# Seven PSUM banks in one tile, waits per bank, and a newly searched order for attention mixed with a spectral filter

## The chip, the cores and the metric

The kernel runs on one core of a Trainium2 chip. Its time is the device time of one execution in microseconds. Times and traces are of the chip; the order in which instructions stand on an engine is read from the built programs, and no duration is taken from there.

## The reference

For one sequence x of 2048 tokens with 448 features, two branches are computed and mixed by a gate per token:

```python
g = sigmoid((x * gate_w).sum(-1, keepdims=True))
# branch A: attention with 16 heads of 28 features
q, k, v = split(x @ wqkv)
p = softmax(einsum("bhqd,bhkd->bhqk", q, k) * 28 ** -0.5)
a = merge_heads(einsum("bhqk,bhkd->bhqd", p, v)) @ wo
# branch B: a filter in the frequency domain
X = rfft2(x) * (w_r + 1j * w_i)
b = irfft2(X)
return g * a + (1 - g) * b
```

All inputs and the output are bf16; 16 x 2048 x 2048 exponentials are needed.

## The kernel before

**Attention.** The 16 heads form four quads g, and the 2048 queries four chunks c of 512: sixteen groups (g, c), taken one after the other. Within a group the 2048 keys are sixteen tiles kt of 128. A *unit* is one head of the quad with one key tile: a matmul of a 32-row tile of TensorE (32x512) that writes 128 keys x 512 queries of scores into one PSUM bank. The four heads of a quad sit on the four row tiles and may run side by side.

There are two ways from scores to weights. In the first (748 units), two units form a *step*: ScalarE (ACT) reads two neighbouring banks in one instruction of 1024 elements per partition and writes exponentials into a ring of 28 slots in SBUF (L1034). There are 374 of these. In the second (69 key tiles, with four units each), VectorE (DVE) adds a constant to the score and stores the sum as 16-bit integers, which are the bits of an approximate exponential (L993), and GpSimd (POOL) makes three copies with shifted bits (L1003); the four versions meet weighted copies of V. After either way, *quads* of four column-tiled matmuls (128x32 weights, 512 columns, pvb<-ring,vw or pvb<-pd,vd) add the product with V, and the row sums, into one bank of PSUM, pvb. At a group's end `normalise` copies pvb out, takes reciprocals, broadcasts them by a DMA through DRAM (rsc, Rb) or at the end by small matmuls, and scales.

**Everything else** runs on the same engines between: projections of q, k and V (xT, wpq, wpk), the transforms as matmuls with tables (CS, A, Bd), the multiplication with the filter (Wg, on DVE), the output projection and the gate (`background`, `out_tile`, `last_tile`).

**PSUM.** Of its eight banks, psA and psB have two each and take steps in turn: step i writes psA if i is even and psB otherwise, so its scores wait for exponential i-2. pvb has one. Three banks (bg) serve all other products by turns, the units for DVE among them; each of these is an `Item`, for which a table says which of the three it gets.

**The order.** The code makes an `Op` for each piece of work, and `run` emits them in the order of a stored table, which was searched beforehand; the engines take their instructions in that order, each engine in its own, and wait on semaphores. Due times and priorities in the code served the search only. Codes from 60000 on are *fillers*: four matmuls with a zero operand that add nothing to pvb. DMAs stand mostly on the queue of SyncE (SP), also in the table's order. All matmuls are recorded with the line of their helper (L432, transposes L435), DMAs with L407.

Of the kernel before, what the change touches and what calls it, by code (L numbers as in the profile page):

```python
# [29 lines left out]
UNITS = 128.0  # L30
# [8 lines left out]
    "eNoN1mNjWEsUQNHxnMG5SW2ltm3bNtPUtm3btm3bto3UdvveX9hf1jakJbHEkXCCJDqJQWKSWCQ2iUPikngkPiEkAUlIEpHEJAkJI0lJMpKc"  # L39
    "UJKCZCApSU6SiniSmuQijHQlQAKiCScZSRoiSXaSlkQlitQk6Ugmkp7UILVINZKNZCG5SVUSheQhWUkOUodkJiVJKRKNlCa1SV5SloSQUFKO"  # L40
    "1Cf5SH5SgBQiBUkxUp6UIRVJYVKEFCXFySZSgWwmlUgJ0oq0JVvIVrKStCPbyHayiqwmVcgOsoZMJGtJZTKJTCZTyFSyjqwnG0g3YpVXG8l0"
    "MoPMJLOIU7PJHDKX7CTziCDzySy/gCwkcWk8Gp8uIovJDL+ELCUJaEK6jKDaRRLRnqQxWU5WkECFqMQ0Ck1Co9JoNDqNQcNoTBqLxqZx6G6y"
    "h+wl+0ioak6iqqfkGXlOXpCXJILcIQ3IfhJJ7pID5B55RV6TKOo+eUMekI7kIXlEHpNo6iCJrqaRGKouOUSS0mQ0pupEYqnkNAU9TJ6Qt2SD"
    "j63ekfckjvpA4qp4qhc5Qo6SlDS+akGOkan0I/lEptHPpAlJoBKq6fQLSaS+Qip6nCRWJ0hqmkR9gxk0TH0lp8hpkoau8WnpGXKWJFX1SG9y"
    "jpwnF8hMepEkU61JOnqJXCZXyFVyjSRX18kNcpOkULfIbZKeplRlaAaakZ4kmWhinoSnUj+hLE2t0qhYvByNzcvTXxCNz/XpVFpVgX6H6Dy9"
    "oqYiHUQyqIzqG0nGm5HvJAaPyX+Qn6Qp+UUyqT+QWf2DSjSLyqo6k+okDk/OK9OGpArtSDvRuDwhX+ezqc60C82uEvD1PhEP439IUp5D/SX/"
    "CKGUMrrac9qV5lSCSqqoprkU0Kw0G81Oc9DcKif9TXLR3NRQS/PQPCovzUdTcEfzKk/z05keaUDj83wqhBagmWlBWogWpkVofpWFhtJ4vCgt"
    "RtuTNqQ47U4LqIw8E+9BS9Ke1PJCyhhtHC+oCqv0vIjiJgMvTaUppoqqtLy4siYlr0p70RKqGi2pqtNSKh0vrVJzYXrTUlSZYaSMKkHT8Bq0"
    "Jk3FmSmrsvFyipi/UF5l5dn5SFpB5eGjaEU1mlZSeXkOPobWopVVB/IbqqiqKhcfS535AdVUTg6mNq2ucvMaqh7tQurTBjQfr0NrKm9qqc+u"
    "MC/DG9J4Bk1dWlsV4XVUDNOI1FUFeEJTkNdTCUwjmpnXV1l4WV6IJzHFeQlegefnFXkDFcs0VDFNXFOTN1KNVWNandfg8U0TVZQnMk1VMhOY"  # L50
    "YryZim1K8lo8jglXIaa5qsRb08o8mklpWqgIVY6X5m1oW9qOtlItVXnenjbjrVUqE86/uaimB2mjEpsmtK1KbkJNO1WVN6XNeQQPM9X4F9de"
    "NeFNeQeV0Xx3P9xP98t1VN1oJ1WX1+MZTDjtoprT7qSz+u0iaBTzx1XhLWhX1ZK2591UJlOKd1cduPQ9lPLpTHrTU/VSrWhtXoeDN9763iqN"
    "6aNa8+imr3I+tRlMve+n0po2vL8aQtE34o35ABX4gSqFSWoym0FqKB1GB6shqi3/6xrwf244JZ76+rwdH6oa8qKG+WGqI2/FC5jhqqDpxkeo"
    "fIb7Qkb4kWqU6sU78eKmO89jSpjRKovpzceoljyr6UvGqh68Jw/xXXkLXsaE+qG8GR2n8prxqjOP7xP4YTyhH8wnqES+iBnC4/i4PrGfqPrQ"
    "SWqyym860C58iipsipmpKokP81F9NN+HT1PZTHRf2cTw09UMNVP15aVNH5LT9KWzVAqf0s9Wa30qH9PH8rF9at+PpvFlzRy1kKb1i+hiOosu"
    "oXPVUprOD+fzVDkzgvfn5c18NYYvUHfoXXqPrqD36QO6ki5UI+gq+pA+oo/pE7qarqFP6SI1lq+l6+h6uoEO4BvpM7pYae/5JjqOL1HP6Qu6"
    "mb6kkXQ8f0WXqtd0C91Kt9FBdDtdpsbT5WoCXaFWquV0IK9kNvoddBwdSEuZQTypX6WS+Yl0El2tZvI1ajKdzquZmmatGs1n8XVqvZrEa5iS"
    "pqLZoPrxyXwG36jm8lF8Np9CJ/A5fCTfpPrTWmYi36yqmwF0Hp/Ct6gKpoqparapZXyrmk13qCW8tgk3c+g0nstsV03MPLpTNTUr+HKewyzl"
    "u1Qzs1vN5xFmj1rE1/LspoVZyTfyxXw+3ac6mTw+r9+rxpCFPJ9fx/P7TfyAmkv3qwK+oG9r2pmD6pA6rPbwOqa1mcqbm728kD+idvBMfifP"
    "7LP4oyqr38wHkGPqFF1AT9Mz9Cw9R7P54+o8vUCz+xz+Ir1EL9MTajW/Qrfwq3QVv0av0xv0pKprbtJTah9fw7uaBby/6WNu0dv0jFrPT6vc"  # L60
    "Zj9vY97QKL6zOad20rNqF91N99DzagPfS/fR/fQAPUgP0QtqFz9Md/Mj9Cg9Ri+q43QZPUFP8kuqgzlJT/GO5hzfzi+ro/wYv6KuqlZmG+9h"
    "eprz/Dg/wa+pLia9v64y+BvqMK9nuptDPLk/wluam+qWus/7mduqgq/oe5mG5gG/o7byC/wir+Qr+7uqij/IQ3goz+jbmwO8kbmnBphu5r6q"
    "6h+om7yaf6j6mt7mPb3C39K7fKCpbx6pW/yxOs3P8idqmhllnqqrfDi5xO/xZ2qcGW/e0RfquXrCL/OyfqIp55/ya3y0eakiVRPfwLxSTf0Y"
    "81rd5s38ZPNGhfs7/AV/q5r7l/ydivAzTDFf3JfwJX0p38K/V/PNB9WflPaRfJB5xT+qT2q2iefL+Bv8DL/OJ5np5rP6ogabIeQRf8af88J+"
    "gvmqvqnH/Av/yhubsaaIf8inmO/qh+JMsE/8p/qlPvOpRjLFNBtK3vJ3/D3/rf6omWaO+av+8n98sVloiP7AP/J/SorlZpYhYoihWgmm+5Hh"
    "huvXfK5ZYRaZN/w3L+qFpuIPlzqnz+V/8G+8oVda6wXmO8/th5lGfpmJKn5y0L+40UvMPPM/SMLqbn6p8drpaMIK1N39SpOE9fA9fS8PLLro"
    "7QO9yYSxpGyECdGhOoZIxvr47aaxj6qFiKKTMycOmW2Gieg6mtYiVHgRQ4OIIraY3SamiCVi6h1mp6nuY+lAxNYJxFGTUMTRIWK/SSJQ1PBx"
    "dZjYZ/aYeDq+TqDjiaEmvqjla/s6vq6v51eZ1SaRSCzq+7giqWjgy/uEerOZ7deYRHqUH+3H+LE+sR7nx/sJfq+ZQE6aOT6JDtNpxFbT0ifV"
    "yXRynVa08W19O9/exxEXTAff0Y80KXRKvc7U9J38QdPKf6Cp9Ef6iaYTqXUanVwcM+nFZ5pWp9OpRGyRXp8xJ8xh84WmFhl0Rl1I7DKFRV/f"
    "z6cQ030ykUmfNwdMZp1FZ9U5RUqRS3T2XXwGsdYcN9l0PnHKZNcD/EA/yGcU+cVgP8Tn0Dl1EXHEFBWnTSaRS2cVQ/1Zk1vHYHl0NnHOxGTD"  # L70
    "fD6dV180XX1mEYtlEbFZft3f3zIFdEEdh2UXf+h685fmEHlEIb3BFNYlxT9aStwx5UURTVgFQVleUVQ/N7lFaXHJFNNTfHE91d8zZcRDU0KX"
    "1DXEffPAlNI1RWldQBQU70w8VkaXFa19OXHbxGfFxHBfVidgI3xCVk1UFIlYdVFOV9Dl9RNTQnyjE/1I/9J8pxV1FVFJ/6A/aRU9yVfWTQVj"
    "03xV8Ys+Mq9NNV1c1Bdf6TNTVTcQv+ld89hU1zV0LVFbTPZPTU0dwmrpSiLSGNZMWPbFvDDzfG093y/wdfRCX1fU0+lZBpaRZWJ1tWOhLAqL"
    "yj6YuOyjWeQvm/o6GsvMGosGuol4axrphnoEaShasEainqgsWrJWrDVrwxKztqwda8+ysSO+sc7OOrAlfqPJwXKyXOyKaaKb6twsD8vLOrJO"
# [1396 lines left out]
```

## Time and profile before

| | |
|---|---|
| median of 3 runs | 380.9 us (380.81 to 381.44) |
| span of the profiled execution | 379.2 us (its time with what lies around the span is not given) |
| granted TensorE clock | 1.000 |
| PE busy | 371.3 us (98%) |
| ACT busy | 351.1 us (93%); the recorded lengths of the 374 exponentials, which overlap, add up to 403.4 us |
| DVE busy | 339.1 us (89%) |
| POOL busy | 234.4 us (62%) |
| first exponential, start of the last | 12.74 us, 364.96 us |

A busy PE includes matmuls whose ends are modelled, so its 98% does not say that it could take nothing more. The length of an exponential in the trace (1.02 us and more) is longer than the distance to the next one, since consecutive ones overlap; its pace is read from starts. A row of the timeline gives start, duration, engine, line, operation, output, inputs and count, and in brackets the idle time before it and what ended that.

### The profile page before, as it was taken

Reading aid. Unit: us, or ns where it says so; the run is one execution under the profiler, and the core shown is the slowest. Engines: PE = TensorE matmul, PEld = TensorE weight load, DVE = VectorE, ACT = ScalarE, POOL = GpSimd, SP = SyncE. Lnnn points to the kernel's source line nnn. Section 1 sums busy time; section 2 is a strip of 40 time slices with the busy share of each in tenths; the row PEclk is TensorE's granted clock in tenths of the full one; section 3 lists DMA queues with packets and bytes.
Section 4 is the critical chain, followed back from the end, with each engine's and each line's share of the span. In section 5 each row is a group of like instructions: output and inputs, shape, how many; then the busy total and the mean of one; then the engine's idle time right before and its main releaser. Section 6 shows DMA issues by size and latency. Waiting matters only on the chain.

```text
span 379.2 us, 12643 instructions
## 1 busy us (share of the span) xinstructions
PE 371.3 (98%) x5117; PEld 142.4 (38%) x5117; DVE 339.1 (89%) x665; ACT 351.1 (93%) x389; POOL 234.4 (62%) x264
## 2 busy tenths in 40 slices
PE   8999999999999999999999999999999999999996
PEld 6634223342433333234333434233333323433564
DVE  1768899999999999999999999999999999988744
ACT  2799999999999999999999999999999999999841
POOL 4446465866778866565553565778597778483510
PEclk9999999999999999999999999999999999999999
DMA  6511101010210112211322212223222122222132
GB/s 145 157 34 44 29 18 36 4 36 2 41 52 22 44 41 54 55 38 30 68 60 93 69 40 49 57 61 70 45 64 74 30 69 72 86 64 72 35 103 75
DMA packets 31158, 21.23 MB, mean 56 GB/s; under 512 B 16260, under 2 KB 29052, under 8 KB 31100
## 3 DMA queue, kind: packets, MB, share of 16 engines
q1 hardware_dynamic: 29708, 19.96, 20.7%
q8 instruction: 40, 0.66, 0.7%
q10 hardware_dynamic: 1392, 0.46, 0.5%
q14 instruction: 18, 0.15, 0.1%
HBM read 14.51 MB, written 1.96 MB: 43 GB/s over the span
## 4 chain that ended last, share of the span: by engine, by line
PE 55%; ACT 31%; issue 6%; DVE 4%; DMA 2%; POOL 1%; SPq 0%; DVEq 0%; ACTq 0%; POOLq 0%
ACT ring L1034 31%; PE bg L432 24%; PE pvb L432 17%; PE psA L432 7%; PE psB L432 6%; DVE pd L993 2%; PE bg L435 1%; DMA CS<-cCS 1%; DVE X L1419 1%; POOL pd L1003 1%; DMA Wg<-in_B_w_i_dram 0%; DVE X L1298 0%; DVE q L1178 0%; DVE t L1362 0%; DVE wpq L1224 0%
## 5 line engine op out<-in xcount | busy, mean ns | idle before, releaser
L1003 POOL INT64_ADD pd<-pd x207 | 211.9, 1038 | 96.7 <-DVE pd L993 27.4
L1034 ACT ACTIVATE ring<-psA 128x1024 bf16<-128x1024 f32 x187 | 201.7, 1078 | 4.7 <-PE psA L432 3.2
L1034 ACT ACTIVATE ring<-psB 128x1024 bf16<-128x1024 f32 x187 | 201.7, 1079 | 2.6 <-PE psA L432 1.4
L993 DVE TENSOR_SCALAR pd<-bg 128x512 uint16<-128x512 f32 x276 | 180.9, 681 | 8.5 <-PE bg L432 3.5
L432 PE MATMUL pvb<-pd,vd 128*32 128x512 bf16 x1104 | 96.9, 384 | 0.1
L432 PE MATMUL bg<-q,k 32*128 32x512 bf16 x276 | 96.3, 383 | 0.2
L432 PEld LDWEIGHTS <-k 32*128 32x128 bf16 x1024 | 40.1, 91 | 122.4 <-issue 117.7
L432 PE MATMUL psB<-q,k 32*128 32x512 bf16 x374 | 73.2, 383 | 1.3 <-ACT ring L1034 0.7
L432 PE MATMUL psA<-q,k 32*128 32x512 bf16 x374 | 72.8, 383 | 0.5 <-ACT ring L1034 0.2
L432 PE MATMUL pvb<-ring,vw 128*32 128x512 bf16 x748 | 67.9, 384 | 0.0
L432 PEld LDWEIGHTS <-vd 128*32 128x32 bf16 x1104 | 25.3, 94 | 35.5 <-issue 31.1
L432 PEld LDWEIGHTS <-vw 128*32 128x32 bf16 x748 | 17.5, 94 | 22.7 <-issue 20.5
L432 PEld LDWEIGHTS <-xT 128*128 128x128 bf16 (+5 forms) x512 | 20.3, 97 | 10.7 <-issue 9.7
L432 PE MATMUL bg<-xT,wpq 128*32 128x512 bf16 (+3 forms) x244 | 21.2, 383 | 0.1
L1362 DVE TENSOR_TENSOR t<-bg,Wg 128x450 bf16<-128x450 f32 x32 | 18.8, 614 | 0.6 <-DMA Wg<-in_B_w_i_dram 0.4
L432 PE MATMUL bg<-xT,wpk 128*32 128x512 bf16 (+2 forms) x240 | 18.9, 383 | 0.0
L432 PE MATMUL bg<-wvr,xT 128*128 128x112 bf16 (+2 forms) x192 | 13.7, 213 | 0.0
L1178 DVE TENSOR_TENSOR q<-pvs,Rb 128x512 bf16<-128x512 f32 x15 | 10.9, 729 | 2.6 <-DMA Rb<-rsc 2.6
L1298 DVE TENSOR_TENSOR X<-bg,oc 128x226 bf16<-128x226 f32 (+1 forms) x32 | 12.3, 386 | 0.5
L432 PEld LDWEIGHTS <-CS 128*32 128x32 bf16 x384 | 9.0, 95 | 9.9 <-issue 5.6
L432 PE MATMUL bg<-xtok,CS 128*32 128x225 bf16 (+1 forms) x192 | 11.2, 294 | 0.7 <-DMA CS<-cCS 0.7
L742 DVE TENSOR_SCALAR k<-bg 128x512 bf16<-128x512 f32 x15 | 10.3, 685 | 1.3 <-PE bg L432 1.1
(117 smaller groups left out, 315.4 us busy)
## 6 DMA issues: line engine op xcount, KB each, us to landing
Rb<-rsc SPq DMA_DIRECT2D x60, 64.0 KB
CS<-cCS SPq DMA_DIRECT2D x16, 192.0 KB
V<-xtok SPq DMA_DIRECT2D x16, 113.0 KB
Wg<-in_B_w_i_dram SPq DMA_DIRECT2D x64, 28.1 KB
xtok<-Ab SPq DMA_DIRECT2D x16, 112.5 KB
xtok<-in_A_x_dram SPq DMA_DIRECT2D x3, 448.0 KB
Wg<-in_B_w_r_dram SPq DMA_DIRECT2D x32, 28.1 KB
out_dram<-wpq SPq DMA_DIRECT2D x6, 112.0 KB
```

The lines of the kernel that those rows point to most:

```text
L432: self.pin(self.nc.tensor.matmul(out, lhsT=lhsT, rhs=rhs, start=start, stop=stop, **kw))
L435: self.pin(self.nc.tensor.transpose(out=out, in_=in_, identity=self.c("ident")[0:n, 0:n]))
L742: self.pin(nc.vector.tensor_scalar(out=dst, in0=self.bgi(it), scalar1=SQ, scalar2=None, op0=ALU.mult))
L993: self.pin(nc.vector.tensor_scalar(out=ys[:, s, :].bitcast(U16), in0=self.bgi(it), scalar1=127 * UNITS, scalar2=0.0, op0=ALU.add, op1=ALU. ...
L1003: self.pin(nc.gpsimd.int64_add(out=fl(pds), in0=fl(ys), in1=PHASE[f] * 0x0001000100010001))
L1034: self.pin(nc.scalar.activation(out=self.ring[:, u0:u0 + len(st), :], in_=slot[:, 0:len(st), :], func=ACT.Exp, scale=LN2 / UNITS))
L1178: e = self.dve(dv(512), lambda: self.pin(nc.vector.tensor_tensor(out=dst, in0=pvs[:], in1=self.Rb[:], op=ALU.mult)), ds, kk, lk=True)
L1298: self.pin(nc.vector.tensor_tensor(out=free_dims(self.X1[:, t, :], [[F, 2], [-1 if dif else 1, n]], (F - 1) * dif), in0=free_dims(self.bgi ...
L1362: self.pin(nc.vector.tensor_tensor(out=out[:], in0=self.bgi(it)[:, 0:F2].rearrange("p (a f) -> p a f", a=2), in1=free_dims(Wg[:], [[F, 2], ...
L1419: self.pin(nc.vector.tensor_tensor(out=free_dims(self.zt[0:FN], [[128, 4], [1, 128]], 512 * t), in0=self.bgi(it)[0:FN, :].rearrange("p (a ...
```

## The change

psA, psB and the three bg banks become one tile, `ps`, of seven banks. Each score unit is now an `Op` with an `Item` of its own, and the table gives it any of the seven banks; the two units of a step must get two neighbouring banks, in either order, and if the second has the lower bank, their slots in the ring are swapped. Since all seven are now one tile, `pin` notes which banks an instruction uses and declares that it does not depend on instructions that use other banks only, unless its `Op` names them as producers. The table has three more parts: the width of each step (2 for all 374), and for each of DVE's key tiles how its four units are grouped: 53 tiles stay at four operations of 512, in 16 one pair of units in neighbouring banks is done by one operation of 1024. The order of all operations and the banks are new. There are no fillers left. The homes of the prologue's products are banks from the table too, and the output tiles 12 and 13 no longer wait by rule for the last exponentials.

The table (a line of each kernel stands for all):

```diff
 TABLE = (
-    "eNoN1mNjWEsUQNHxnMG5SW2ltm3bNtPUtm3btm3bto3UdvveX9hf1jakJbHEkXCCJDqJQWKSWCQ2iUPikngkPiEkAUlIEpHEJAkJI0lJMpKc"
...
+    "eNpjYhoF9AcAJW4C7Q==",
...
 def unpack(table):
     raw = [zlib.decompress(base64.b64decode(t)) for t in table]
-    return np.frombuffer(raw[0], np.uint16).tolist(), np.frombuffer(raw[1], np.uint8).tolist()
+    return [np.frombuffer(r, t).tolist() for r, t in zip(raw, (np.uint16, np.uint8, np.uint8, np.uint8))]
...
+    def need(self):
+        return [p for d in self.op_now.deps for p in d.made]
...
     def run(self, filler):
         items = [o.acq for o in self.ops if o.acq is not None]
-        codes, banks = unpack(TABLE)
-        for it, b in zip(items, banks):
+        assert len(items) == len(self.banks)
+        for it, b in zip(items, self.banks):
             it.bank = b
-        for c in codes:
+        for c in self.codes:
             if c < FILL0:
+                self.used, self.op_now = set(), self.ops[c]
                 self.ops[c].emit()
+                self.used = set()
...
     def pin(self, ins):
...
+        if self.sc.used:
+            used = frozenset(self.sc.used)
+            keep = [p for p, u in self.sc.need() if not used & u]
+            if ins.ins.engine in self.before:
+                keep.append(self.before[ins.ins.engine])
+            for other in self.bank_sets:
+                if not used & other:
+                    self.tc.declare_no_dep(ins.ins, group="bank" + repr(sorted(other)), reason="other banks",
+                                           keep=[k for k in keep if k.name in self.bank_sets[other]])
+            self.bank_sets.setdefault(used, set()).add(ins.ins.name)
+            self.tc.add_to_no_dep_group("bank" + repr(sorted(used)), ins.ins)
+            self.sc.op_now.made.append((ins.ins, used))
+        self.before[ins.ins.engine] = ins.ins
         return ins
...
-        self.psA = ps.tile([P, 2, 512], F32, name="psA")
-        self.psB = ps.tile([P, 2, 512], F32, name="psB")
+        self.ps = ps.tile([P, 7, 512], F32, name="ps")
         self.pv = ps.tile([P, 512], F32, name="pvb")
-        self.bgt = [ps.tile([P, 512], F32, name=f"bg{i}") for i in range(3)]
...
     def bgi(self, item, dt=F32):
-        t = self.bgt[item.bank][:]
+        t = self.ps[:, item.bank, :]
+        self.sc.used.add(item.bank)
         return t if dt == F32 else t.bitcast(dt)
...
+            for part in self.PARTS[sc.parts[di]]:
...
+                def f1(part=part, its=its, ys=ys, at=at):
+                    bs = sorted(it.bank for it in its)
+                    sc.used.update(bs)
+                    w, e = len(bs), part[-1] - part[0]
+                    assert w == 1 or bs[1] == bs[0] + 1
+                    if its[0].bank > its[-1].bank:
+                        at[part[0]], at[part[1]] = part[1], part[0]
+                    self.pin(nc.vector.tensor_scalar(
+                        out=free_dims(ys[:], [[512 * e, w], [1, 512]], 512 * part[0]).bitcast(U16),
+                        in0=self.ps[:, bs[0]:bs[0] + w, :],
+                        scalar1=127 * UNITS, scalar2=0.0, op0=ALU.add, op1=ALU.max))
...
         for i, st in enumerate(self.steps):
-            slot = self.psA if i % 2 == 0 else self.psB
-            deps = [exps[i - 2]] if i >= 2 else []
+            deps, ms = [], []
...
-            def fe(st=st, slot=slot, u0=u0):
-                self.pin(nc.scalar.activation(out=self.ring[:, u0:u0 + len(st), :], in_=slot[:, 0:len(st), :],
+            def fe(st=st, u0=u0):
+                us = sorted(st, key=lambda u: uit[u].bank)
+                bs = [uit[u].bank for u in us]
+                assert all(b == bs[0] + j for j, b in enumerate(bs))
+                self.sc.used.update(bs)
+                for u, slot in zip(us, sorted(self.unit_slot[u] for u in us)):
+                    self.unit_slot[u] = slot
+                self.pin(nc.scalar.activation(out=self.ring[:, u0:u0 + len(st), :],
+                                              in_=self.ps[:, bs[0]:bs[0] + len(st), :],
                                               func=ACT.Exp, scale=LN2 / UNITS))
```

In the changed kernel the helper's lines are L464 (matmul), L467 (transpose) and L439 (DMA), DVE's approximate exponential is L1025. Three places show how the order moved. The first is PE around the 162nd exponential, where projections, the transform and attention run together; q_85, k_89 and vw_91 before are q_81, k_85 and vw_87 now, and ps stands for any of the seven banks. Before:

```order
L432 LDWEIGHTS k_89
L432 MATMUL bg_65<-q_85,k_89 128x512
L432 LDWEIGHTS k_89
L432 MATMUL psB<-q_85,k_89 128x512
...
L432 MATMUL psA<-q_85,k_89 128x512
...
L432 LDWEIGHTS vw_91
L432 MATMUL pvb<-ring,vw_91 32x512
```

Now:

```order
L464 MATMUL pvb<-ring,vw_87 32x512
L464 LDWEIGHTS k_85
L464 MATMUL ps<-q_81,k_85 128x512
...
L464 LDWEIGHTS A
L464 MATMUL ps<-X_127,A 32x450
```

Both visits have five score units, four for ACT and one for DVE: before, DVE's comes first, then psB's two and psA's two; now the two of one step, DVE's unit, and the two of the next. What follows moved from a product with V to a piece of the transform.

The second is DVE in the stage where the filter is applied, with a merged operation; t and Z are the filter's products, pd the approximate exponentials. Before:

```order
L1369 TENSOR_TENSOR Z_149<-t_147 128x225
L1367 TENSOR_TENSOR Z_149<-t_145 128x225
L993 TENSOR_SCALAR pd_107<-bg_65 128x512
L1362 TENSOR_TENSOR t_144<-bg_64,Wg_142 128x450
L1362 TENSOR_TENSOR t_146<-bg_64,Wg_142 128x450
L993 TENSOR_SCALAR pd_111<-bg_66 128x512
```

Now:

```order
L1408 TENSOR_TENSOR Z_144<-t_142 128x225
L1406 TENSOR_TENSOR Z_144<-t_140 128x225
L1025 TENSOR_SCALAR pd_104<-ps 128x512
L1025 TENSOR_SCALAR pd_109<-ps 128x1024
L1025 TENSOR_SCALAR pd_109<-ps 128x512
```

Two of four units of the key tile that pd_109 holds are done in one operation, between units of another key tile.

The third is SP's queue at the last loads of the transform's table CS; Wg is the filter, rsc and Rb the reciprocals of a group. Before:

```order
L407 DMA Wg_142<-in_B_w_r_dram 64x1x225
L407 DMA Wg_143<-in_B_w_r_dram 64x1x225
L407 DMA CS_140<-cCS 128x768
L407 DMA Wg_142<-in_B_w_i_dram 64x1x225
L407 DMA CS_141<-cCS 128x768
L407 DMA Rb<-rsc_128 32x512 x2
```

Now:

```order
L439 DMA Wg_139<-in_B_w_r_dram 64x1x225
L439 DMA CS_136<-cCS 128x768
L439 DMA Wg_138<-in_B_w_i_dram 64x1x225
L439 DMA Wg_139<-in_B_w_i_dram 64x1x225
L439 DMA rsc_124<-rr_102 128x16
L439 DMA CS_137<-cCS 128x768
```

The loads of Wg still stand ahead of the first CS; between the two CS there are now another Wg load and the store of the reciprocals.

297 lines of the change are left out of this document (151 added, 146 removed).

## The prediction

> **What bounds the kernel now.** I read the span in seven stages first: for each stage its length, then the busy time of PE, PEld, DVE, ACT and POOL with instruction counts, the granted clock, the share of the DMA engines and GB/s.
>
> ```profile
> 12.70:28.50 15.80, 15.72 (x202) 7.17 (x204) 11.63 (x22) 14.92 (x19) 6.16 (x10) 1.00 0.21 49
> 28.50:50.70 22.20, 22.17 (x274) 7.30 (x266) 19.38 (x38) 22.20 (x27) 13.15 (x23) 1.00 0.12 31
> 50.70:153.80 103.10, 102.27 (x1421) 35.36 (x1417) 99.98 (x198) 103.06 (x114) 75.11 (x77) 1.00 0.13 33
> 153.80:201.40 47.60, 47.60 (x684) 17.46 (x677) 46.28 (x90) 44.95 (x50) 26.29 (x27) 1.00 0.21 51
> 201.40:341.90 140.50, 138.24 (x1801) 49.16 (x1802) 135.52 (x276) 140.19 (x154) 98.03 (x98) 1.00 0.25 63
> 341.90:366.00 24.10, 24.10 (x452) 11.16 (x448) 16.13 (x26) 20.94 (x23) 9.23 (x9) 1.00 0.24 69
> 366.00:379.20 13.20, 9.67 (x244) 7.02 (x236) 6.80 (x12) 1.55 (x2) 0.00 (x0) 0.99 0.22 72
> ```
>
> No engine bounds all of it. ACT, which computes the 374 exponentials, is idle for 0.00, 0.04 and 0.31 us in the second, third and fifth stage: 266 of the 379 us in which nothing on PE, DVE or POOL can shorten the run unless ACT itself has less to do. PE has no idle time in the fourth and sixth stage, and ACT has 2.65 and 3.16 us there (the length less its busy time). In the first ACT misses 0.88 us. The last 13.2 us have no exponential; there PE and what hangs on it count. The clock is full throughout, so it explains nothing.
>
> Next, what ends ACT's waits (line, what it waited for: us in all, times, longest), and the same for PE's score matmuls.
>
> ```profile
> ACT ring L1034 <- PE psA L432: 4.5, 8, 0.8
> ACT ring L1034 <- PE psB L432: 2.5, 6, 0.6
> ...
> PE psB L432 <- ACT ring L1034: 0.7, 2, 0.4
> ...
> PE psA L432 <- ACT ring L1034: 0.2, 1, 0.2
> ```
>
> So ACT waits 7.0 us for scores, but PE waits only 0.9 us for an exponential to give a score bank back. Scores are late because PE is at other work, not because a bank is missing. Two of ACT's waits, and the last ones, in its timeline (start, duration, and in brackets the idle time before it and what ended it):
>
> ```profile
> 161.44 1.08 ACT L1034 ACTIVATE ring<-psA 128x1024 bf16<-128x1024 f32 x1
> 162.85 1.02 ACT L1034 ACTIVATE ring<-psB 128x1024 bf16<-128x1024 f32 x1 [0.32 <-PE psB L432]
> 163.77 1.02 ACT L1034 ACTIVATE ring<-psA 128x1024 bf16<-128x1024 f32 x1
> ...
> 361.50 1.02 ACT L1034 ACTIVATE ring<-psA 128x1024 bf16<-128x1024 f32 x1 [0.69 <-PE psA L432]
> 362.42 1.02 ACT L1034 ACTIVATE ring<-psB 128x1024 bf16<-128x1024 f32 x1
> 364.04 1.02 ACT L1034 ACTIVATE ring<-psA 128x1024 bf16<-128x1024 f32 x1 [0.61 <-PE psA L432]
> 364.96 1.02 ACT L1034 ACTIVATE ring<-psB 128x1024 bf16<-128x1024 f32 x1
> ```
>
> An undisturbed exponential follows its predecessor after 0.92 us (362.42 less 361.50); the one at 162.85 came after 1.41. Last, the chain that ended last, whose shares confirm the picture: about half PE, a third ACT.
>
> ```profile
> PE 55%; ACT 31%; issue 6%; DVE 4%; DMA 2%; POOL 1%; SPq 0%; DVEq 0%; ACTq 0%; POOLq 0%
> ```
>
> **The base of the sum.** The page gives this execution's span, 379.2 us, and no time around it; the median of the three runs is 380.9. I change the span and add the 1.7 us between the two again.
>
> **Part 1, PE's work.** The exponentials are the same 374 of 1024 elements, POOL's copies the same 207, and the matmuls that compute are the same; PE loses only the 24 zero matmuls of six fillers. What the new order changes is how the row-tiled score units (32x512) alternate with the column-tiled rest. PE's timeline prices it:
>
> ```profile
> 160.24 0.40 PE L432 MATMUL pvb<-ring,vw 128*32 128x512 bf16 x4
> 160.47 0.39 PE L432 MATMUL bg<-xT,wpq 128*32 128x512 bf16 x4
> 160.79 0.39 PE L432 MATMUL psA<-q,k 32*128 32x512 bf16 x2
> 160.85 0.37 PE L432 MATMUL bg<-q,k 32*128 32x512 bf16 x1
> 161.15 0.40 PE L432 MATMUL pvb<-pd,vd 128*32 128x512 bf16 x4
> 161.38 0.39 PE L432 MATMUL bg<-xT,wpq 128*32 128x512 bf16 x4
> ```
>
> A column quad follows a column quad after 0.23 us (160.24 to 160.47, 161.15 to 161.38), a score round follows a quad after 0.32 (160.47 to 160.79), and a quad follows a score round after 0.30 to 0.36. A change of mode therefore costs 0.10 us. Counted from the two orders, changes of mode fall from 717 to 691 (26 x 0.10 = 2.6 us), rounds of score units from 387 to 379 (8 x 0.22 = 1.8 us), and the fillers take 0.6 to 1.6 us, bounded by half of a quad's 0.22 and by their recorded length:
>
> ```profile
> L432 PE MATMUL pvb<-zero x24: 219/259/283, 251.3 to 277.9; 128*32 128x256 bf16 x12, 128*32 128x192 bf16 x8, 128*32 128x128 bf16 x4
> ```
>
> (six quads by 0.10 or 0.26). PE gains 5.0 to 6.0 us; I take 5.4. What matters is where. I counted rounds and changes between the same exponentials in both orders and priced them as above: about 1.1 us go before 50 us, 0.3 comes in between 50 and 154, nothing changes between 154 and 201, 4.0 go between 201 and 342, and 0.7 go from the 351st exponential to the end. (These are sums of counts by the starts above, no runs.) The 4.0 lie in the stage where ACT has 0.31 us of idle time. They are worth at most that.
>
> **Part 2, the heavy stage (153.8 to 201.4).** PE is full and its work stays the same. The possible gain is all of ACT's idle time, 2.65 us, if PE could be ahead of ACT when the stage begins; the possible loss comes with part 4. What seven interchangeable banks give directly is that a score unit need not wait for the exponential before the last. That wait is 0.9 us in the whole trace. I take 0.4 of it as gained, half, since by the table of banks 580 of the 744 units still take over a bank that the exponential two before gave back, and only 27 one that an older exponential did.
>
> **Part 3, head, transfer wait and tail.** In the head one exponential is late by 0.8 us because a block of projections stands before its scores; the new order has such a block there too. I count 0, and keep 0.9 either way. At 305 us PE waits for a table of the transform (chain of waits, then ACT's timeline):
>
> ```profile
> 301.95 3.92 DMA CS<-cCS
> 305.91 0.69 PE bg L432 x5
> ...
> 305.34 1.12 ACT L1034 ACTIVATE ring<-psB 128x1024 bf16<-128x1024 f32 x1
> 306.74 1.02 ACT L1034 ACTIVATE ring<-psA 128x1024 bf16<-128x1024 f32 x1 [0.28 <-PE psA L432]
> ```
>
> The exponential came 1.40 after its predecessor instead of 0.92: 0.5 us. SP issues in order, and this transfer stands behind a run of filter loads. In the new order it is still behind seven or more of them, but from the release of its buffer to its use there are now 4 exponentials, not 3: about 3.7 us against a transfer of 3.9. So it may be just late still. I take 0.2 of the 0.5. The tail: the work left on PE after the last score falls from 10.7 to 9.8 us by the same count, and from the 351st exponential on from 34.3 to 33.6. PE bounds here and it ends the chain, so I take 0.7; the bounds are 0 (the gaps of the last 13.2 us, 3.5, grow by as much) and 1.6 (half of these gaps go too).
>
> **Part 4, the exponentials on DVE.** 16 of 69 key tiles have one pair of 512-wide operations merged into one of 1024. From DVE's timeline:
>
> ```profile
> 120.55 0.68 DVE L993 TENSOR_SCALAR pd<-bg 128x512 uint16<-128x512 f32 x1
> 121.15 0.38 DVE L1298 TENSOR_TENSOR X<-bg,oc 128x224 bf16<-128x224 f32 x1
> 121.45 0.24 DVE L1169 RECIPROCAL rr<-rs 128x16 f32<-128x16 f32 x1
> ```
>
> 512 elements hold DVE for 0.60 us (120.55 to 121.15), 224 for 0.30, so 288 more cost 0.30 and 512 more about 0.53: a merged one 1.13 instead of 1.20, 0.07 saved, or 1.1 us for all sixteen. The bounds are 0 and 0.60 each (9.6 us), the first since the pair can at worst cost twice one. The skill's "Perfetto Trace Analysis", Optimizing Scalar/DVE Operations, puts the fixed part of a DVE operation on PSUM at about 125 ns; by that sixteen merges save 2.0 us. Either is off the path wherever ACT bounds, and is cover lost where it matters: both units must be there before it starts, and the first bank comes free 0.53 us later. 131 of the 744 score units of the exponentials now take a bank that DVE read last; before it was 2. Where DVE is late, PE waits with everything behind it, since its instructions are in order: other scores, the products with V, and the transform. DVE is busy 46.28 of 47.60 us in the heavy stage, so it has no slack to speak of there. For the likeliest case I count 0: laid end to end with the durations above, DVE's results that come less than 0.2 us ahead of the PE instruction that needs them are 22 in the new order and 17 in the old, few among some hundreds. The loss is the second rival.
>
> **Sum.** 0.4 (banks) + 0.2 (transfer) + 0.7 (tail) + 0.1 (what ACT can still gain in its own stages, a third of 0.31) = 1.4 us. 379.2 - 1.4 + 1.7 = 379.5 us, with 378.0 to 380.1 as this case's own range.
>
> **Rivals.** (a) *No change.* The tail's 0.7 goes into its gaps and ACT's 7 us stay where PE is full. For it: no stage in which PE bounds has less of the work but the tail. Against: the tail's order is really shorter by 0.9 us at the end. It gives 380.7, and all from 380.1 to 381.7, 0.2% either side, which a measurement of this kernel can't tell from no change.
>
> (b) *Slower: scores wait for DVE.* The place is the two stages in which PE is full, 153.8 to 201.4 and 341.9 to 366.0; 71.7 of the 352 us in which exponentials run, so about 27 of the 131 units. A unit that comes while DVE is at the operation before its own waits between 0 and 0.60 us, 0.3 in the mean; PE passes it on one to one, as it has no idle time. A third of the 27 being late costs 2.7, all of them 8.1. From five late units on (5 x 0.3 = 1.5) the gain is gone. With 13 late: 379.5 + 3.9 = 383.4; with a third, 382.2. For it: DVE's 97% in that stage, and the merges, which hold a bank longer. Also the work of PE between two scores is less even in the new order in the heavy stage and the tail, which makes ACT wait where there was no wait. Against: the order places a unit on a DVE bank mostly where DVE read long before. I take 382.3 for this case.
>
> (c) *The whole of ACT's waits.* If the scores came early enough everywhere, ACT's 0.88, 2.65, 0.31 and 3.16 us would go, 7.0, and the tail's 0.7: 373.2; with half of the waits, 376.7. For it: any of seven banks can take a score while both earlier exponentials run. Against: PE is busy 47.60 of 47.60 there, and no bank gives it time. "Perfetto Trace Analysis" of the Trainium skill, Optimizing Tensor Performance, wants independent matmul groups rotated through different PSUM banks, so that evacuation overlaps the next group, and under Matmul Optimizations all 8 banks used; by it (c) is the case, while the row of PE's waits (0.9 us) says the overlap is there already.
>
> (d) *The waits aren't per bank.* If each instruction waited for the last one on the whole tile, an exponential could not run beside the next scores, and its 0.92 would grow by a score's 0.39: 374 x 0.39 = 146 us, 527 in all. The wait lists of the changed order name single earlier instructions, so 0.01.
>
> **Chances.** Forecast 0.36, (a) 0.28, (b) 0.25, (c) 0.10, (d) 0.01. Faster by over 0.2% (below 380.1) is forecast and (c), 0.46; within it 0.28; slower (over 381.7) 0.26. The range: down to 376.2, which leaves the better half of (c) out, and up to 383.2, beyond a late third of the units and near 13 late ones.
>
> **What would show it.** Right: ACT's waits for scores still 5 to 7 us and in the same two stages; PE with more idle time between 201 and 342 us and that stage as long as before; the last exponential within a microsecond of 366.0 and the end 12.5 us after; DVE's operation of 1024 taking 1.1 to 1.2 us. Wrong: waits of PE for DVE on score units beyond 1 us in all, or the stage 153.8 to 201.4 longer (b); that stage at 46 us or less, and the last exponentials without gaps (c). The forecast fails most easily if the small gaps of the heavy stage, which depend on the neighbours of each score and not on sums, close or open throughout.

## The result and the profile after

The changed kernel takes 393.9 us (393.52 to 394.31), the kernel before beside it 380.86: a ratio of 1.0343 (95% interval 1.0328 to 1.0357), 13.0 us slower. 379.5 had been forecast, and the range ended at 383.2. The profiled execution's span is 392.1 us instead of 379.2. Two of e6's four runs below, 408.3 and 408.8 us, lie over 1.5% above its fastest and are left out of its time and ratio.

The page of the changed kernel, first two parts:

```profile
PE 372.6 (95%) x5093; PEld 142.9 (36%) x5093; DVE 347.5 (89%) x649; ACT 353.3 (90%) x389; POOL 235.1 (60%) x264
...
PEclk9999899999999999999799999999999999999998
```

No engine has more work to speak of but DVE, with 8.4 us more in fewer instructions (649 for 665). And the granted clock, full throughout before, now falls in two places, besides the very end. What ACT and PE waited for (line, what for: us, times, longest):

```profile
ACT ring L1075 <- PE ps L464: 17.4, 24, 3.3
...
PE ps L464 <- DVE pd L1025: 2.8, 9, 0.7
PE pvb L464 <- DVE vd L914: 2.2, 1, 2.2
PE ps L464 <- DVE vt L905: 1.8, 1, 1.8
PE ps L464 <- ACT ring L1075: 1.7, 5, 0.5
```

ACT waits 17.4 us for scores, 7.0 before. PE, which waited 0.2 us for DVE before, now waits 6.8 in the three groups shown, and two single waits make 4.0 of that.

The starts of the exponentials, read from ACT's timeline of both kernels and numbered from 0, say where the time went:

| from number to number | before, us | after, us | difference |
|---|---|---|---|
| 5 to 29 | 22.48 | 22.82 | +0.34 |
| 29 to 34 | 4.51 | 9.45 | **+4.94** |
| 34 to 60 | 23.78 | 23.80 | 0.0 |
| 60 to 152 | 84.84 | 86.76 | +1.92 |
| 152 to 175 | 22.63 | 22.59 | 0.0 |
| 175 to 180 | 4.56 | 9.01 | **+4.45** |
| 180 to 204 | 24.27 | 24.42 | +0.15 |
| 204 to 310 | 97.25 | 98.46 | +1.21 |
| 310 to 340 | 28.29 | 27.50 | -0.79 |
| 340 to 373 | 34.12 | 34.61 | +0.49 |
| 373 to the end | 14.23 | 14.16 | -0.07 |

(Number 5 starts at 18.23 us before and at 18.48 now.) Two stretches of five exponentials hold 9.4 of the 13 us. In stages (length, busy time of PE, PEld, DVE, ACT, POOL, clock, DMA share, GB/s) they are the second and the fourth row:

```profile
11.70:41.00 29.30, 26.57 (x339) 12.04 (x335) 22.45 (x40) 26.79 (x32) 13.56 (x25) 1.00 0.23 59
41.00:50.30 9.30, 6.48 (x66) 1.92 (x64) 6.93 (x10) 4.78 (x6) 3.32 (x8) 0.82 0.01 3
50.30:178.00 127.70, 125.77 (x1725) 42.05 (x1722) 122.75 (x233) 126.12 (x139) 83.39 (x86) 1.00 0.13 34
178.00:194.00 16.00, 14.24 (x164) 5.76 (x156) 14.25 (x23) 11.66 (x14) 8.79 (x9) 0.79 0.14 37
...
212.00:352.00 140.00, 135.56 (x1758) 48.88 (x1747) 136.41 (x265) 139.13 (x153) 97.96 (x100) 1.00 0.23 64
```

At the first place, PE's timeline of the changed kernel (start, duration, what; idle time before it in brackets):

```profile
40.76 0.39 PE L464 MATMUL ps<-q,k 32*128 32x512 bf16 x2
43.36 0.40 PE L464 MATMUL pvb<-pd,vd 128*32 128x512 bf16 x4 [2.21 <-DVE vd L914]
...
46.45 1.93 PE L464 MATMUL ps<-xT,wpq 128*32 128x512 bf16 x16
...
49.22 1.04 PE L464 MATMUL ps<-xT,wpq 128*32 128x512 bf16 x16
```

DVE's timeline of the same time:

```profile
38.35 0.61 DVE L905 TENSOR_TENSOR vt<-ps,w 128x448 f32<-128x448 f32 x1
39.07 4.24 DVE L914 TENSOR_SCALAR vd<-vt 128x580 bf16<-128x580 f32 x1
43.23 1.27 DVE L1025 TENSOR_SCALAR pd<-ps 128x512 uint16<-128x512 f32 x2
```

And POOL's:

```profile
38.96 0.37 POOL L557 COPY wpq<-X 96x224 bf16<-96x224 bf16 x1
39.30 2.05 POOL L1039 INT64_ADD pd<-pd  x2
41.30 0.37 POOL L557 COPY wpk<-X 96x224 bf16<-96x224 bf16 x1
41.65 1.03 POOL L1039 INT64_ADD pd<-pd  x1
42.62 0.37 POOL L554 COPY wpk<-X 128x224 bf16<-128x224 bf16 x1
42.94 0.60 POOL L554 COPY wpq<-X 128x224 bf16<-128x224 bf16 x1
43.49 0.24 POOL L843 CAST vw<-w 128x16 bf16<-128x16 f32 x1
```

One DVE operation, a scaling of V from SBUF to SBUF (vd<-vt), takes 4.24 us; of the other fifteen of the same shape twelve take 0.44 to 0.47, and three 0.66 to 1.30. It ends at 43.31 us, in the last 0.4 us of a row of POOL's operations that has had no gap since 35.64. PE waits 2.2 us for it. Sixteen matmuls that take 1.04 us at 49.22 took 1.93 at 46.45: between them the clock was half. At 184 us it is the same with other operations: products of the transform (Z) take 1.1 us each instead of 0.27, and the queries' scaling takes 1.5 instead of 0.7, all during a row of POOL's copies; PE waits 1.8 us, and from 185.2 to 192.0 its clock is half.

Before, POOL's copies were kept away from such operations. That stood in a view of the kernel before that the prediction didn't use, POOL's waits:

```profile
POOL pd L1003 <- DVE q L1178: 9.0, 7, 2.4
...
POOL pd L1003 <- DVE vd L888: 8.2, 5, 2.1
POOL pd L1003 <- DVE Z L1367: 6.7, 6, 3.1
POOL pd L1003 <- DVE sq L747: 6.3, 6, 2.2
POOL pd L1003 <- DVE Z L1369: 5.5, 4, 2.9
```

POOL's copies (pd<-pd) read none of q, vd, Z or sq. They waited 35.7 us for them all the same, because `pin` makes a POOL instruction wait for the last DVE operation marked `lk` that was emitted before it (the lines with `self.port`). Both kernels have these lines. But the wait goes one way: a DVE operation that is emitted behind a row of POOL's copies is not protected if the copies run late. In the new order the scaling of V stands behind fourteen operations of POOL, and twelve of those started late, at 35.64 us, after a wait of 3.5 us for DVE.

### The profile page after: what moved, and what is told of

Read it like the earlier page. It is cut to its first block, busy times and chain, and to the rows that moved or that the text cites. A ratio compares the mean times of both kernels' runs of the same rounds, so it can differ in the third digit from the quotient of the medians.

```text
span 392.1 us, 12526 instructions
## 1 busy us (share of the span) xinstructions
PE 372.6 (95%) x5093; PEld 142.9 (36%) x5093; DVE 347.5 (89%) x649; ACT 353.3 (90%) x389; POOL 235.1 (60%) x264
## 4 chain that ended last, share of the span: by engine, by line
PE 58%; DVE 18%; ACT 11%; DMA 4%; POOL 4%; issue 3%; SPq 1%; ACTq 0%; DVEq 0%; POOLq 0%
PE ps L464 38%; PE pvb L464 19%; ACT ring L1075 10%; DVE pd L1025 8%; POOL pd L1039 4%; DVE vd L914 2%; DMA xtok<-in_A_x_dram 2%; SPq L439 1%; DVE sq L773 1%; DMA X<-in_A_wqkv_dram 1%; DVE t L1401 1%; PE ps L467 1%; DVE X L1337 1%; DVE pvs L1205 1%; DVE Z L1408 1%
## 5 line engine op out<-in xcount | busy, mean ns | idle before, releaser
L1075 ACT ACTIVATE ring<-ps 128x1024 bf16<-128x1024 f32 x374 | 348.1, 1079 | 18.2 <-PE ps L464 17.4
L1025 DVE TENSOR_SCALAR pd<-ps 128x512 uint16<-128x512 f32 (+1 forms) x260 | 178.9, 714 | 7.7 <-PE ps L464 6.4
L464 PE MATMUL ps<-q,k 32*128 32x512 bf16 x1024 | 147.8, 386 | 6.2 <-DVE pd L1025 2.4
L464 PE MATMUL pvb<-pd,vd 128*32 128x512 bf16 x1104 | 96.7, 386 | 3.0 <-DVE vd L914 2.2
L464 PEld LDWEIGHTS <-k 32*128 32x128 bf16 x1024 | 38.9, 91 | 123.3 <-issue 118.8
L464 PE MATMUL pvb<-ring,vw 128*32 128x512 bf16 x748 | 68.1, 389 | 0.9 <-DVE pvs L1205 0.8
L464 PEld LDWEIGHTS <-vd 128*32 128x32 bf16 x1104 | 25.3, 94 | 40.7 <-issue 33.1
L464 PEld LDWEIGHTS <-vw 128*32 128x32 bf16 x748 | 17.6, 95 | 22.9 <-issue 20.3
L464 PEld LDWEIGHTS <-xT 128*128 128x128 bf16 (+5 forms) x512 | 20.6, 98 | 13.5 <-issue 12.3
L464 PE MATMUL ps<-xT,wpq 128*32 128x512 bf16 (+3 forms) x248 | 20.9, 398 | 0.3 <-DVE wpq L554 0.3
L1401 DVE TENSOR_TENSOR t<-ps,Wg 128x450 bf16<-128x450 f32 x32 | 19.0, 614 | 0.9 <-issue 0.5
L464 PE MATMUL ps<-xT,wpk 128*32 128x512 bf16 (+3 forms) x244 | 18.7, 383 | 0.0
L464 PE MATMUL ps<-wvr,xT 128*128 128x112 bf16 (+2 forms) x192 | 14.3, 220 | 2.0 <-DVE vt L905 1.8
L464 PEld LDWEIGHTS <-CS 128*32 128x32 bf16 x384 | 9.3, 95 | 9.5 <-issue 5.4
L1337 DVE TENSOR_TENSOR X<-ps,oc 128x226 bf16<-128x226 f32 (+1 forms) x32 | 12.2, 387 | 0.5
L914 DVE TENSOR_SCALAR vd<-vt 128x580 bf16<-128x580 f32 x16 | 12.5, 806 | 0.2
L464 PE MATMUL ps<-Bd,xT 128*32 128x226 bf16 (+2 forms) x256 | 12.2, 263 | 0.2 <-DVE pd L1025 0.2
L464 PE MATMUL ps<-wpq,q 128*32 128x448 bf16 x128 | 11.9, 364 | 0.0
## 6 DMA issues: line engine op xcount, KB each, us to landing
CS<-cCS SPq DMA_DIRECT2D x16, 192.0 KB
```

Of the source, the lines that this page charges most:

```text
L464: self.pin(self.nc.tensor.matmul(out, lhsT=lhsT, rhs=rhs, start=start, stop=stop, **kw))
L914: self.pin(nc.vector.tensor_scalar(out=free_dims(self.vd[g][:], [[32, n4], [1, DH + 1]], 128 * (DKT * f + o4)), in0=free_dims(self.vt[:], ...
L1025: self.pin(nc.vector.tensor_scalar(out=free_dims(ys[:], [[512 * e, w], [1, 512]], 512 * part[0]).bitcast(U16), in0=self.ps[:, bs[0]:bs[0] ...
L1075: self.pin(nc.scalar.activation(out=self.ring[:, u0:u0 + len(st), :], in_=self.ps[:, bs[0]:bs[0] + len(st), :], func=ACT.Exp, scale=LN2 / ...
L1337: self.pin(nc.vector.tensor_tensor(out=free_dims(self.X1[:, t, :], [[F, 2], [-1 if dif else 1, n]], (F - 1) * dif), in0=free_dims(self.bgi ...
L1401: self.pin(nc.vector.tensor_tensor(out=out[:], in0=self.bgi(it)[:, 0:F2].rearrange("p (a f) -> p a f", a=2), in1=free_dims(Wg[:], [[F, 2], ...
```

## The experiments

Theory P: DVE's operations between SBUF and SBUF can't run while POOL's copies do, the new order lets them meet, PE starves, and then its clock is halved. Theory B, the prediction's second rival: score units wait for banks that DVE gives back late. Beside these stood the suspicion that the one tile and its declared waits cost something.

**e1, the old order in the new code.**

```diff
-TABLE = (codes, banks, widths, parts of the changed kernel)
+TABLE = (codes of the old order with fillers, psA -> 0, 1, psB -> 2, 3, bg -> 4..6, widths 2, parts 0)
```

> The changed code (one tile of seven banks, waits per bank, score units as operations of their own) with the old kernel's order, the old banks (psA as 0 and 1, psB as 2 and 3, bg as 4 to 6), no merged DVE operation and the old fillers. If the new order alone costs the 13 us (theory P: DVE operations that read and write SBUF are held up by runs of POOL's copies, PE starves and its clock is halved): as before, 380 to 382 us. If the tile and its declared waits cost something themselves: well above, up to 394.

380.99 us, ratio 0.999 (0.9977 to 1.0003). The tile, the declared waits and the single score units cost nothing and bring nothing; all 13 us come from the order, the banks and the merges.

**e2, no merged operations.**

```diff
-parts: 16 of 69 tiles with a merged pair
+parts: none; both halves stand where the merged one stood
```

> The changed kernel with its order and banks, but each of the 16 merged DVE operations of 1024 made two of 512 that stand at the same place. Theory P: no gain, 392 to 396 us, since the stalls at 41 and 184 us have nothing to do with the merges. Theory B (the second rival of the prediction: scores wait for banks that DVE gives back late, the merged ones latest): 2 us or more are gained, 392 at most, and PE's waits for DVE on score units shrink from 2.8 us.

395.37 us, ratio 1.0372 (1.0345 to 1.0399), against 1.0343 with the merges. They are no cause; if anything they help by the 1.1 us that sixteen of them save DVE. Theory B's part on merges is out. PE's waits show the same two single ones:

```profile
PE ps L466 <- DVE pd L1027: 3.1, 10, 0.7
PE pvb L466 <- DVE vd L916: 2.2, 1, 2.2
PE ps L466 <- DVE vt L907: 1.8, 1, 1.8
```

**e3, two moves in the order.**

```diff
 POOL: ... copy, copy, wpq, copy, wpq
-POOL: copy, copy, wpk, copy, wpk, wpq, vw        (ahead of the scaling of V)
 DVE:  vd (first scaling of V)
+POOL: copy, copy, wpk, copy, wpk, wpq, vw        (behind it)
...
-DVE:  sq, Z, Z, sq, q, vt
+DVE:  sq, sq, q, vt, Z, Z
```

> The changed kernel with two small moves in the order: seven operations of POOL (three copies of 1024, four small ones) now stand behind the first scaling of V (the DVE operation that took 4.24 us at 39.1) and wait for it; and two products of the transform on DVE (1.1 us each at 181 to 183) now stand behind the queries' scaling and the copy of V that PE waits for at 184. Theory P: the scaling takes 0.5 us, PE does not stall at 41, its clock stays full there, 5 us are gained; at 184 another 3 to 4.4: 384 to 387 us. Theory B: no more than 1 us is gained, 392 or more.

390.41 us, ratio 1.0234 (1.0213 to 1.0254). At the first place the theory holds; the scaling takes 0.57 us (DVE's timeline of e3), POOL waits 0.42 for it, and the clock stays full:

```profile
38.93 0.57 DVE L916 TENSOR_SCALAR vd<-vt 128x580 bf16<-128x580 f32 x1
```

The stages of e3 at both places:

```profile
38.00:50.00 12.00, 11.57 (x146) 3.51 (x144) 11.07 (x18) 11.57 (x13) 8.63 (x13) 1.00 0.01 3
180.00:184.00 4.00, 2.05 (x25) 1.13 (x27) 4.00 (x7) 1.84 (x3) 2.53 (x3) 1.00 0.04 7
184.00:188.00 4.00, 4.00 (x37) 0.77 (x36) 3.47 (x7) 2.73 (x3) 0.00 (x0) 0.57 0.25 55
```

Exponentials 29 to 34 took 5.26 us instead of 9.45. At the second place my move failed: the products of the transform were held up in their new place just as before (0.85 and 1.10 us), PE waited 1.7 us for DVE there, and the clock fell again (0.57). Numbers 175 to 180 took 8.89, 0.1 less. Moving what is held up moves the stall, it doesn't remove it.

**e4, fillers in the stalls.**

```diff
+PE: 18 x filler(256 columns) ahead of the product that waits for vd
+PE: three score units, then 14 x filler, ahead of the last product before the stall at 184 us
```

> The changed kernel with zero matmuls that add nothing: 18 fillers of 256 columns ahead of the product that waits at 41 us, and 14 in the stall at 184 (three score units put ahead of them), so that PE is busy while it waits. POOL's and DVE's order is the same. If PE's halved clock is a share of the loss (theory P): the clock stays full, and 3 to 5 us of the 13 are gained, 389 to 391 us, though the DVE operation still takes 4 us. If only the stalls count and the clock is a side effect: 393 or more.

390.48 us, ratio 1.0243 (1.0222 to 1.0265). DVE and POOL did as in the changed kernel; the scaling of V again took 4.24 us. But PE was busy with zeros, as its timeline of e4 shows,

```profile
41.60 2.15 PE L466 MATMUL pvb<-zero 128*32 128x256 bf16 x72
43.89 0.40 PE L466 MATMUL pvb<-pd,vd 128*32 128x512 bf16 x4
```

and the clock stayed at 1.00 in both places (stages of e4):

```profile
44.00:50.00 6.00, 5.39 (x71) 1.93 (x67) 5.12 (x11) 3.91 (x5) 1.45 (x4) 1.00 0.00 0
...
184.00:192.00 8.00, 7.76 (x120) 3.07 (x108) 7.90 (x17) 6.20 (x7) 2.36 (x3) 1.00 0.15 35
```

Numbers 29 to 34 took 7.90 us (9.45), 175 to 180 6.88 (9.01): 3.7 us of the 9.4 are the halved clock that follows the stalls, not the stalls. (At the second place the fillers came with another move, three score units ahead of a product; but ACT runs the six exponentials up to the stall in 5.61 us without a gap with and without it, so this moved nothing that shows.)

**e5, POOL moved at both places.**

```diff
 DVE:  vd (first)
+POOL: copy, copy
 DVE:  vd (second), vd (third)
+POOL: wpk, copy, wpk, wpq, vw
...
-POOL: vw, copy, copy, copy
 DVE:  sq, sq, q, vt, Z, Z
+POOL: vw, copy, copy, copy
```

> The changed kernel with more moves of the same kind: the two copies after the first scaling of V and the rest of that run of POOL's after the third scaling; at 184 us the two products of the transform behind the scalings that PE waits for, as in e3, and now also POOL's three copies and one small operation behind these products. Theory P: no DVE operation is held up at either place, PE does not stall for more than 0.6 us, the clock stays at 1.00, and both losses of 4.9 and 4.4 us go: 393.9 - 9.3 = 384.6, between 383.5 and 386. If the second stall has another cause (the order of PE there, or the filter's products): 388 to 390 as e3.

386.83 us, ratio 1.0162 (1.0141 to 1.0183): 7.1 of the 13 gained, not 9.3; the expected range was missed by 0.8. The first place is as before the change (4.53 us for numbers 29 to 34, 4.51 before). At the second Z takes 0.27 again and the clock is full, but earlier copies still hold two operations up (DVE's timeline of e5):

```profile
175.70 1.74 DVE L775 TENSOR_TENSOR sq<-q 128x512 bf16<-128x512 bf16 x2
177.37 1.52 DVE L1219 TENSOR_TENSOR q<-pvs,Rb 128x512 bf16<-128x512 f32 x1
178.81 0.61 DVE L907 TENSOR_TENSOR vt<-ps,w 128x448 f32<-128x448 f32 x1
179.34 0.27 DVE L1408 TENSOR_TENSOR Z<-t 128x225 bf16<-128x225 bf16 x1
```

so numbers 175 to 180 still take 6.0 us instead of 4.56.

**e6, the old kernel without POOL's waits.**

```diff
     def dve(self, dur, fn, deps, key, rel=0.0, free=None, name="dve", lk=False):
-        o = self.sc.op("DVE", dur, self.ported(fn) if lk else fn, deps, key, rel, free=free, name=name)
+        o = self.sc.op("DVE", dur, fn, deps, key, rel, free=free, name=name)
```

> The old kernel, in which POOL waits for the DVE operation that was emitted last before it and reads and writes SBUF (a wait that no data needs), with these waits left out; order, banks and work are the old ones. Theory P: POOL's copies now start while such DVE operations are due, and these (scalings of V and of queries, squares, products of the transform) take 0.5 to 3 us longer here and there, PE waits for them: 382 to 390 us. If POOL's copies don't hold DVE up, POOL loses 30 us of waits and the time is 379 to 381.

399.0 us (397.66 and 400.26), ratio 1.0477 (1.043 to 1.0525). That is well above the 390 I had allowed. The opposite of the rival's gain: the waits that no data needs are worth some 18 us to the old order. One of the two kinds of products of the transform is held up in the middle case, not only now and then (the group's count, and shortest, middle and longest duration in ns):

```profile
L1367 DVE TENSOR_TENSOR Z<-t x16: 266/766/1111, 184.9 to 330.0; 128x225 bf16<-128x225 bf16 x16
```

**e7 and e8, both orders with short copies.** POOL's copies keep their place and their waits but handle an eighth of the elements, so that most of the second to fourth versions of DVE's exponentials is left out.

```diff
-    self.pin(nc.gpsimd.int64_add(out=fl(pds), in0=fl(ys), in1=...))
+    self.pin(nc.gpsimd.int64_add(out=fl(pds)[:, 0:64], in0=fl(ys)[:, 0:64], in1=...))
...
+    for p in self.pd:
+        self.pin(nc.vector.memset(p[:], 0.0))
```

> The old kernel with POOL's copies cut to an eighth of their elements (64 of 512 words of 64 bits), so that it leaves out most of the second, third and fourth versions of DVE's exponentials; the buffers are zeroed by DVE at the start, before its first input is there. Orders and waits are the old ones. It is the base for e8. Theory P: POOL's waits for DVE stay, nothing was held up for long in the old kernel, so about as before: 378 to 381.5 us.

> The changed kernel with the same cut of POOL's copies to an eighth and the same zeroing (so it, too, leaves out most of three of four versions). Theory P: nothing is held up on DVE, both stalls and the small ones go, the clock stays at 1.00; 12 of the 13 us go but for what the order itself costs in lumps on PE, 1 to 3 us more than e7: 379.5 to 384. If the order's lumps on PE or late banks are the cause, 8 us or more above e7 stay: 387 or more.

387.44 and 387.47 us: with short copies the two orders take the same time. Both are later than I expected because the zeroing, nine operations of 0.91 us, took longer than DVE's idle time at the start and delayed the first exponential, to 19.12 and 19.57 us from 12.74. So I compare what follows the exponential number 5, up to the span's end. (The first exponential is no good base: it starts at 12.74 us before and at 11.74 in e1, which has the same order, but number 5 at 18.23 and 18.30.) Old order: 361.0 us with full copies (379.2 - 18.23) and 361.1 with short ones (385.7 - 24.61). New order: 373.6 (392.1 - 18.48) and 362.0 (387.1 - 25.07). Of 12.6 us, 11.7 go when the copies are short. The 0.9 that stay may belong to the order or to the execution, since the profiled one of e8 is the slowest of its four (388.85 us). No scaling of V, square, product or scaling of queries is held up by more than 0.1 us any more, and PE's waits for DVE behind the start are down to 1.4 us (e8, all lines over 0.1):

```profile
PE ps L466 <- DVE pd L1027: 0.5, 3, 0.2
PE pvb L466 <- DVE pvs L1207: 0.4, 1, 0.4
PE ps L466 <- DVE k L770: 0.3, 1, 0.3
PE ps L466 <- DVE xT L738: 0.2, 1, 0.2
```

Short copies also bring POOL's own results earlier. That isn't where the time went: in the changed kernel PE waits only 0.5 us for POOL's copies, and none of DVE's listed waits is for them.

**e9, the old kernel without its fillers.**

```diff
-TABLE codes with six fillers
+TABLE codes without them
```

> The old kernel without its six fillers (at 251, 253 and 278 us), all else the same. They take 0.6 to 1.6 us of PE in a stage where ACT bounds. Theory P: PE is never idle for 1.7 us there, so the clock stays at 1.00 without them too and nothing changes: 380.5 to 381.5. If they guard the clock: it falls there and the time rises by 2 us or more.

381.23 us, ratio 1.0002 (0.9987 to 1.0018): no change, as theory P has it. Where PE doesn't starve, zeros do nothing.

Put side by side: for each run the time by which DVE's operations of the five kinds (vd, sq, the two Z, q) exceeded their usual length in the profiled execution, added up, and the span from number 5 on.

| kernel | held up, us | number 5 to the end, us |
|---|---|---|
| before | 1.9 | 361.0 |
| after | 11.7 | 373.6 |
| e5, POOL moved | 8.3 | 366.1 |
| e6, old order without POOL's waits | 19.6 | 380.1 |
| e7, old order, short copies | 0.0 | 361.1 |
| e8, new order, short copies | 0.2 | 362.0 |

(Usual length: 0.45, 0.42, 0.27, 0.27 and 0.68 us; differences under 0.05 are left out.) The time follows what is held up, but not in proportion: e5 loses little with 8.3 us, since what it holds up is seldom what PE waits for.

The "SBUF — State Buffer" page of the Trainium skill, SBUF: two separate sides, has a rule for this: DVE and GpSimd share one pair of SBUF ports, as an exclusive lock that is held for a whole instruction, taken by DVE operations in a two-port mode or with two SBUF inputs. The runs agree: operations with an input in PSUM keep their length beside POOL's copies (vt 0.61 us at 184.80 in the changed kernel, during one, and 0.61 at 178.81 in e5, during none), and so do all 161 of DVE's exponentials of 512 that run beside the copies in the changed kernel (0.69 us at most, as the 69 that run beside nothing of POOL's). The five kinds above, with inputs in SBUF only, do not keep it; the small reciprocals (rr<-rs, 0.24 us), with one SBUF input, do. Whether the scaling, with one SBUF input too, runs in a two-port mode no run here shows.

## Why the prediction was wrong

**The sum.** The step that failed is in part 4: "For the likeliest case I count 0", and with it the base of the whole sum, which took every DVE duration from the trace of before as a constant. The sum had no term for an operation that takes longer because of what POOL does at that time. That term is 11.7 of 12.6 us (e7 and e8): about 3.7 of halved clock at two places, 5.7 that stay there with a full clock (the stalls and what hangs on them), and the rest spread over the long stages, as between numbers 60 and 152 (86.76 us, 84.48 in e8). The rows that could have given it were POOL's waits of the kernel before: 35.7 us for results that POOL never reads, and the code says why. I counted 22 against 17 tight results of DVE and took that for the risk; what counts is which DVE operations stand behind a row of POOL's copies.

**Part 1.** Right in what it said: 5.4 us of PE's work were worth nothing. With short copies, the new order from number 5 on is 0.9 us longer than the old, not shorter (e7, e8).

**Part 2.** The 0.4 us for freer banks didn't come: PE's waits for exponentials went from 0.9 to 1.7 us, five of them. And e1 shows that the tile by itself changes nothing. The heavy stage lost 4.4 us in one place and was as before around it.

**Part 3.** The head, counted as 0, was right: number 5 starts 0.25 us later. PE's wait for the transform's table is gone from its waits, as half expected, but not because the order mends it: in the changed kernel a unit waits 0.7 us for DVE some eight exponentials earlier, and with short copies the wait for the table is back (0.7 us in e8, 0.6 in e7). The tail's 0.7 us was mis-sized in sign: from number 340 to the end it is 0.42 us longer. PE does have less to do after the last score (8.70 us in the last 13.1 instead of 9.67 in 13.2), but its gaps grew by as much, and the last exponentials wait more: the bound of 0 that I gave was too kind. e8, where nothing is held up, has the same tail, so it is the order's own.

**Part 4's merges** were sized right: two rows of DVE's timeline of the changed kernel give the distance,

```profile
179.31 1.23 DVE L1025 TENSOR_SCALAR pd<-ps 128x1024 uint16<-128x1024 f32 x1
180.45 0.56 DVE L773 TENSOR_TENSOR sq<-q 128x512 bf16<-128x512 bf16 x1
```

1.14 us against the 1.13 worked out from rows; so a merge saves 0.06 us where 0.07 was counted.

**The rivals.** (b) had the sign, and the way in which it gets through: PE in order behind one late DVE result. It had the wrong reason (how long DVE holds a bank; e2 refutes the merges, and with the same banks but short copies PE's waits for DVE's exponentials fall from 2.8 us to 0.5: DVE was late, the choice of banks only passed it on), one of its two places, and a time of 382.3 us where 393.9 came, since it had neither the operations that are held up nor the clock. (c) and (d) are out, the latter by e1. Two of the rivals' times don't follow from their own sums, which decided nothing: (a) gives 380.9 (379.2 + 1.7), not 380.7, and (b) 382.2 (379.5 + 2.7), not 382.3. "The clock is full throughout, so it explains nothing" was true of the trace of before and wrong as a guide: it was full in an order in which PE never waited longer than 0.7 us once exponentials ran.

## What to carry to other kernels

Durations of a trace hold for its own order: before a new order is priced, look for waits that no data needs, since they show which operations must not meet, and check for each such pair who now stands behind whom, and what happens if one of them is late. A wait that protects in one direction only is as good as the plan's timing. And price a starved PE with its clock: here the two stretches with a stall of about 2 us and half the clock behind it lost 4.9 and 4.5 us. Not every such stall is followed by it, as the last section shows.

## What the runs showed of the hardware

**A scaling can wait through several of POOL's instructions.** The 4.24 us at 39.07 go past three copies of POOL (1.03 us each) and the small ones between them; one in e6 took 2.45, and two scalings in e3 took 2.12 us together, 1.2 more than alone. Operations with two SBUF inputs (Z, sq, q) never lost more than about 0.9 us in any run, less than one copy of POOL. By the rule of "SBUF — State Buffer" of the Trainium skill, SBUF: two separate sides, the one that starts first has the ports for the instruction; that a scaling is held up through several of POOL's instructions, one after the other, it doesn't say; nor does the trace show whether the scaling stood still or crept along. Why the two kinds differ wasn't tried.

**The clock.** It is half or full, nothing between, in half-microsecond windows of the changed kernel but for those in which it turns. By the trace's record of it, it is half from 45.23 to 48.65 us, after the stall that begins at 41.15, and from 185.18 to 192.01, after the one at 183.71: for 3.41 us and for twice that (windows around the second):

```profile
185.00:185.50 0.50, 0.04 (x1) 0.04 (x1) 0.50 (x2) 0.00 (x0) 0.50 (x1) 0.68 0.00 0
185.50:191.00 5.50, 5.50 (x44) 2.07 (x43) 4.42 (x9) 3.07 (x3) 1.28 (x2) 0.50 0.16 42
...
192.00:192.50 0.50, 0.50 (x11) 0.10 (x3) 0.50 (x2) 0.50 (x1) 0.00 (x0) 0.99 0.00 0
```

From 185.5 on PE was busy without a break at half rate, 6.5 us, longer than the 3.4 us of activity after which "TensorE: Matmul & The Clock Gate" of the Trainium skill, Part 1, has the gate open again; its remark that the window runs freely would allow up to twice that, 6.8 us (an estimate from that page), which fits the length.

Not every stall halves the clock, and the traces show which do. In all eleven, the recorded changes of the clock lie whole multiples of 3.41 us apart. Cut each trace into such pieces, and while exponentials run the clock falls at the end of a piece in which PE was idle for 1.48 us or more (2.15 and 1.48 in the changed kernel, 1.79 and 1.76 in e2, 1.95 in e3, 1.74 in e6), and after none with 1.23 or less. A stall that lies across a border counts in two pieces. So in e6 a stall of 1.74 us at 249.66, within one piece, was followed by half the clock, and one of 2.01 us at 180.16, which lies in two, was not (windows of e6, cut at these borders):

```profile
177.98:181.39 3.41, 2.18 (x34) 0.84 (x32) 3.41 (x4) 2.76 (x3) 2.88 (x4) 1.00 0.24 48
181.39:184.80 3.41, 2.63 (x33) 1.10 (x33) 3.41 (x7) 2.12 (x3) 0.27 (x1) 1.00 0.02 5
249.66:253.07 3.41, 1.67 (x18) 0.43 (x18) 3.41 (x7) 1.52 (x3) 3.00 (x3) 1.00 0.31 75
253.07:259.90 6.83, 6.83 (x58) 1.44 (x55) 4.38 (x8) 5.69 (x6) 2.92 (x3) 0.50 0.03 5
```

Where exactly the limit lies is open: after the last exponential a piece with 1.61 us idle (e2) was not followed by half the clock. Open too is why it came back after one piece at 45.23 and only after two at the second place of e2 and in e6, where PE was busy all through the first.
